# Another order of all operations in a scheduled kernel: pooled attention and a gated-convolution feed-forward on one core

## The chip, the core and the metric

The kernel runs on one core of a Trainium2 chip. The core has a matrix engine (TensorE, PE in the profile; PEld is its weight load), a vector engine (VectorE, DVE), a scalar engine (ScalarE, ACT), a general engine (GpSimd, POOL) and a sync engine (SyncE, SP) that here only issues DMAs. Each engine takes its instructions in the order in which they were written, and waits on semaphores where it needs another's result. The metric is the device time of one execution in microseconds (us); lower is better.

## What is computed

The input has 8 batches, 8 heads, 576 rows and 64 columns per head. Keys and values are averaged over 8 neighbouring rows, so that 72 are left; then follow the softmax attention and a feed-forward net whose gate is a convolution over 3 rows:

```python
k_p = k.reshape(B, H, Sp, pool, D).mean(axis=3)
v_p = v.reshape(B, H, Sp, pool, D).mean(axis=3)
scores = scale * np.matmul(q, k_p.transpose(0, 1, 3, 2))
attn = np.exp(scores - np.max(scores, axis=-1, keepdims=True))
attn = attn / (np.sum(attn, axis=-1, keepdims=True) + 1e-09)
x = np.matmul(attn, v_p)                    # heads joined: (8, 576, 512)
h = np.maximum(x @ w_in, 0.0)               # 512 -> 1024
conv_out = sum over k of conv_w[k] * h shifted by k - 1 rows
out = (h * sigmoid(conv_out)) @ w_out       # 1024 -> 512, f32
```

## The kernel before

**Tiling.** The batches go in pairs, as groups 0 to 3. A group has nine attention tiles of 128 rows (group 0 has ten). A tile runs through this chain: scores on PE (lines 607 and 620), the row maximum on DVE (633), its subtraction on DVE (645; for group 0 on PE, 653), the exponential on ACT (682), a transpose of the weights (groups 0 and 1 on PE, 692, with a copy; groups 2 and 3 by a DMA transpose that SyncE issues, `att_send`, 701), the product with the values on PE (717), the reciprocal of the sums on DVE (730), the division on ACT or DVE (738, 745), and a transpose of the result (on PE, 762, with a copy, 770; for the later batches by DMA, `att_out`, 754).

**Feed-forward.** Per batch PE multiplies by w_in in eight blocks fb of 128 columns, each in two halves (775); ACT takes the relu (784). The convolution is made on PE for some blocks (939) and for the rest, in batches 4 to 7, by taps on DVE (911) with the tanh on ACT (921). Taps need a halo: for these batches the first and last rows of pairs of blocks are copied by POOL or ACT (`ffn_wrap`, 859 and 860). DVE makes the gate (979, 981) and multiplies by h, four blocks at once (`ffn_times`, 989). Then PE multiplies by w_out, per tile in two halves (997); ACT or DVE copies the PSUM bank to memory (`ffn_copy`, 1008) and a DMA of two parts of 128 KB stores it (`ffn_store`, 1020), from SyncE or, for some tiles of group 3, from ACT.

**Loads.** SyncE and ACT load the first pieces of batch 0, which are cast by ACT or DVE (306). All the other loads are issued by POOL, which casts on the way: queries (284, into one of four buffers qp), keys by pairs of batches (291, into the only buffer kk), values (317 and 320, into three buffers v), w_in (327) and w_out (335). Values and keys are then pooled on DVE (511, 515, 464) and keys on PE (431, 470, 493). Queries are transposed on PE (541, with a copy, 559), except those of batches 6 and 7: these go through a DMA transpose that SyncE issues (`q_send`, 553).

**Spare matmuls.** `fill` (424) multiplies constants and writes to a PSUM bank that nobody reads.

**What sets the order.** All operations are made first, as a list, with their buffers left open. `Graph.order` (line 164) then walks a table of numbers, `ORDER`: a negative number takes a spare matmul, another number n takes operation n // 2 on the first or second of its possible engines, by n % 2. Two more tables are read along the way: `FORMS` (the shape in which an operation uses the matrix array) and `PLACES` (the buffer or bank that each result takes). The operations are emitted in this order, so it is the order of the instructions on each engine, and it also sets which buffer is reused when. The tables are constants; no planner runs.

## Time and profile before

| | us |
|---|---|
| three runs, median (lowest to highest) | 213.52 (213.04 to 213.94) |
| the profiled execution | 213.68 |
| its span, first to last instruction or transfer | 211.7 |
| PE busy | 198.9 |
| DVE busy | 190.5 |
| ACT busy | 167.2 |
| POOL busy | 36.7 |

The profile's time axis begins with the span, and all times of instructions below are on it. Busy time counts an engine's instructions, not their issue of DMAs. PE has work from 2.8 to 205.9 us. A row of a group gives the line, the engine, the operation, what it writes and reads, and a count; then the busy time, the mean of one in ns and the idle time ahead of them, with what ended it.

### The profile page before, as it was taken

The numbers are of one execution on the slowest core, as the hardware profiler recorded it, in microseconds if no ns is written. First come the engines' busy times: TensorE is split into PE (matmuls) and PEld (weight loads), VectorE is DVE, ScalarE is ACT, GpSimd is POOL, SyncE is SP. The second block draws the span as 40 slices with busy tenths as digits, with TensorE's granted clock in tenths as the row PEclk, the third lists the DMA queues.
The fourth block names the chain that finished last, engine by engine and source line by source line (L and its number), as shares of the span: only waits on it lengthen the run. The fifth ranks groups of instructions, "written<-read, shape, count | busy, mean of one in ns | idle before, by whom it ended". The sixth has DMA issues, their size and how long they took to land.

```text
span 211.7 us, 6644 instructions
## 1 busy us (share of the span) xinstructions
PE 198.9 (94%) x2726; PEld 136.4 (64%) x2746; DVE 190.5 (90%) x338; ACT 167.2 (79%) x345; POOL 36.7 (17%) x60
## 2 busy tenths in 40 slices
PE   4899999999999999999999899999999999999990
PEld 1468788765688876776778675666666656654450
DVE  7879988999999999999998989999999999999520
ACT  2558677998999869999979977989899997889030
POOL 8604630052131110200000021000014400202000
PEclk9999999999999999999999999999999999999997
DMA  6999999999999999879663646756646626204985
GB/s 212 222 205 206 208 206 208 208 207 205 208 206 208 202 179 202 177 139 156 130 92 69 147 96 78 173 104 151 122 96 133 113 64 149 53 0 103 261 259 171
DMA packets 48834, 33.47 MB, mean 158 GB/s; under 512 B 28300, under 2 KB 43812, under 8 KB 48804
## 3 DMA queue, kind: packets, MB, share of 16 engines
q0 software_dynamic: 15216, 15.40, 44.6%
q1 hardware_dynamic: 32432, 15.93, 35.9%
q10 hardware_dynamic: 1156, 1.72, 2.8%
q8 instruction: 21, 0.34, 0.6%
q14 instruction: 9, 0.07, 0.1%
HBM read 32.52 MB, written 9.44 MB: 198 GB/s over the span
## 4 chain that ended last, share of the span: by engine, by line
PE 68%; DVE 19%; issue 5%; ACT 4%; DMA 2%; DVEq 0%; ACTq 0%
PE psum L997 25%; PE psum L775 22%; PE psum L717 5%; PE psum L939 3%; DVE negm L633 3%; DVE v L511 2%; PE psum L692 2%; DMA eT<-e 2%; PE psum L424 2%; DVE sd L645 2%; DVE gT L981 2%; PE psum L620 2%; DVE gT L989 1%; PE psum L653 1%; PE psum L762 1%
## 5 line engine op out<-in xcount | busy, mean ns | idle before, releaser
L775 PE MATMUL psum<-xT,w_in_sb 128*128 128x288 bf16 x512 | 72.0, 286 | 0.2
L997 PE MATMUL psum<-w_out_sb,gT 128*128 128x512 bf16 (+1 forms) x276 | 65.6, 373 | 1.4 <-issue 0.6
L775 PEld LDWEIGHTS <-w_in_sb 128*128 128x128 bf16 x512 | 47.8, 98 | 15.3
L784 ACT ACTIVATE hT<-psum 128x576 bf16<-128x576 f32 x64 | 41.1, 669 | 8.0 <-PE psum L775 7.8
L997 PEld LDWEIGHTS <-gT 128*128 128x128 bf16 x296 | 27.5, 98 | 26.5 <-DVE gT L989 0.5
L633 DVE TENSOR_REDUCE negm<-psum 128x8 f32<-128x576 f32 (+2 forms) x37 | 27.4, 750 | 2.0 <-ACT e L682 0.9
L921 ACT ACTIVATE gT<-tg,ratio 128x576 bf16<-128x576 f32 x28 | 21.6, 795 | 2.2 <-DVE tg L911 2.1
L911 DVE SCALAR_TENSOR_TENSOR tg<-hT,ratio,tg 128x576 f32<-128x576 bf16 x28 | 22.3, 813 | 0.7
L911 DVE SCALAR_TENSOR_TENSOR tg<-hT,ratio 128x576 f32<-128x576 bf16 x28 | 22.2, 812 | 0.2 <-ACT gT L921 0.2
L859 POOL COPY hT<-hT 128x126 bf16<-128x126 bf16 x7 | 5.7, 808 | 93.8 <-ACT hT L784 74.9
L989 DVE TENSOR_TENSOR gT<-gT,hT 128x2304 bf16<-128x2304 bf16 x16 | 21.6, 1354 | 0.2
L645 DVE TENSOR_TENSOR sd<-psum,negm 128x576 f32<-128x576 f32 x27 | 19.9, 751 | 0.6
L717 PE MATMUL psum<-vm,eT 128*128 128x65 bf16 (+5 forms) x240 | 19.0, 222 | 0.9 <-DMA eT<-e 0.9
L738 ACT ACTIVATE x<-psum,r 128x64 bf16<-128x64 f32 (+1 forms) x80 | 17.6, 352 | 2.8 <-DVE r L730 2.7
L682 ACT ACTIVATE e<-sd 128x576 bf16<-128x576 f32 x27 | 18.6, 703 | 0.4 <-DVE sd L645 0.2
L745 DVE TENSOR_TENSOR x<-psum,r 128x512 bf16<-128x512 f32 (+1 forms) x27 | 18.2, 682 | 0.5
L717 PEld LDWEIGHTS <-eT 128*128 128x128 bf16 (+1 forms) x240 | 15.1, 100 | 5.3 <-DMA eT<-e 1.7
L939 PE MATMUL psum<-hT,dw 64*64 64x288 bf16 (+2 forms) x576 | 17.0, 256 | 0.3 <-ACT qT L559 0.2
L939 PEld LDWEIGHTS <-dw 64*64 64x64 bf16 x576 | 13.9, 107 | 3.4 <-issue 2.3
L424 PE MATMUL psum<-gT 128*128 128x448 bf16 x40 | 13.1, 433 | 3.2 <-DVE gT L1106 2.8
L1008 ACT COPY osb<-psum 128x512 f32<-128x512 f32 x24 | 14.3, 600 | 1.2 <-PE psum L997 1.2
L511 DVE TENSOR_TENSOR v<-v 128x1280 bf16<-128x1280 bf16 (+2 forms) x24 | 12.9, 538 | 0.2
(95 smaller groups left out, 244.8 us busy)
## 6 DMA issues: line engine op xcount, KB each, us to landing
out_dram<-osb SPq DMA_DIRECT2D x54, 128.0 KB, 2.5
v<-in_v_dram POOLq DMA_DIRECT2D x8, 512.0 KB, 12.6
qp<-in_q_dram POOLq DMA_DIRECT2D x7, 576.0 KB, 15.3
kk<-in_k_dram POOLq DMA_DIRECT2D x3, 1152.0 KB, 13.7
out_dram<-qp ACTq DMA_DIRECT2D x12, 128.0 KB, 3.4
hT<-in_k_dram SPq DMA_DIRECT2D x2, 576.0 KB, 5.2
w_in_sb<-in_moe_w_in_dram POOLq DMA_DIRECT2D x2, 512.0 KB, 13.7
w_out_sb<-in_moe_w_out_dram POOLq DMA_DIRECT2D x1, 1024.0 KB, 23.7
```

The source lines that it names most:

```text
L633: nc.vector.tensor_reduce(out=a["m"][0:rows], in_=a["s"][0:rows, :, 0:2 * KW].rearrange("p a (h s) -> p a h s", s=Sp), axis=AX.X, op=OP.ma ...
L645: nc.vector.tensor_tensor(out=a["d"][0:rows], in0=a["s"][0:rows, :, 0:2 * KW].rearrange("p a (h s) -> p a h s", s=Sp), in1=a["m"][0:rows]. ...
L682: nc.scalar.activation(out=dst, in_=src, func=ACT.Exp,)
L717: nc.tensor.matmul(out=a["o"][lo:hi, h // 4, (h % 4) * (D + 1):(h % 4 + x1 - x0) * (D + 1)], lhsT=a["eT"][:, j, lo:hi], rhs=buf("vm", b)[: ...
L745: nc.vector.tensor_tensor(out=a["x"][0:rows].rearrange("p (a h d) -> p a h d", a=2, d=D), in0=ov[:, :, :, 0:D], in1=r[0:rows].unsqueeze(3) ...
L775: nc.tensor.matmul(out=banks(ps)[:, j, 0:SC], lhsT=w_in_block(dc, fb), rhs=buf("xT", g)[:, dc, i * S + j * SC:i * S + (j + 1) * SC], start ...
L784: nc.scalar.activation(out=h_of(b)[:, fb].rearrange("p (a s) -> p a s", a=2), in_=banks(ps)[:, :, 0:SC], func=ACT.Relu, scale=1.0 if (b, f ...
L911: nc.vector.scalar_tensor_tensor(out=acc, in0=h, scalar=w, in1=acc if tap else mid, op0=OP.mult, op1=OP.add)
L921: nc.scalar.activation(out=gate, in_=acc_of(b, fb, ps), func=squash(b, fb), scale=ratio[:, 1, fb:fb + 1])
L939: nc.tensor.matmul(out=banks(pss[r ^ c])[c * D:(c + 1) * D, j, lo:hi], lhsT=dw[r * D:(r + 1) * D, tap * n_fb + fb, :], rhs=hT[r * D:(r + 1 ...
L989: nc.vector.tensor_tensor(out=gate, in0=gate, in1=h_of(b)[:, four], op=OP.mult)
L997: nc.tensor.matmul(out=bank(ps)[0:rows, columns], lhsT=buf("gT", g)[:, fb, t * P:t * P + rows], rhs=w_out_sb[:, fb, columns], start=(fb == 0),
```

## The change

The three tables `ORDER`, `FORMS` and `PLACES` have other values; everything else is the same. Both versions of `ORDER` have 1077 entries, 40 of them spare matmuls. 38 operations are on another engine: DVE makes two fewer copies of transposed queries and eight instead of five of the late copies of the output, which ACT loses, and the two casts of batch 0's raw keys are swapped between ACT and DVE; the rest are single small operations. Some operations have another form, so that PE has 2740 matmuls instead of 2746. The first lines of the table, as the diff has them:

```diff
-        0, 12, 10, 24, 16, 4, 44, 28, 8, 36, 14, 32, 46, 19, -1, -1, -1, -1, 21, 7,
-        -1, -1, -1, 42, 48, 26, 34, 38, 64, 2, -1, -1, -1, 40, -1, -1, -1, -1, -1, 114,
-        102, 108, 118, 122, 126, 104, 117, 113, 111, 107, 120, 292, 128, 125, -1, -1, -1, 66, 68, 358,
...
+        0, 12, 10, 24, 16, 4, 44, 28, 8, 36, 14, 32, 46, 42, 40, 3, 48, 26, -1, 38,
+        19, 66, -1, -1, -1, 64, 34, 6, 68, -1, -1, 21, -1, -1, 74, -1, -1, -1, 114, 102,
+        107, 118, 104, 108, 111, 113, -1, -1, -1, 116, 120, 292, 294, 58, 122, 126, -1, 296, -1, 125,
...
```

What it moves is seen in the instructions of each engine. Names are buffers with their numbers; x2 is two instructions of one kind.

**The start, on ACT.** The first instructions of ACT before; kk0 takes the raw keys of batch 0 (staged in hT0), qp2 its raw queries (staged in hT1):

```order
L1116 ACT_TABLE_LOAD
L1116 CAST gT1_122<-ident_62 128x128
L324 DMA gT1_122<-in_moe_conv_w_dram 24x128
L306 CAST qp2_76<-hT1_117 128x2x256 x2
L306 CAST kk0_78<-hT0_116 128x1152
L559 COPY qT0_79<-psum_61 128x2x256
L456 CAST kT0_82<-psum_61 64x2x72 x3
L559 COPY qT0_79<-psum_61 128x2x320
L682 ACTIVATE e3_101<-psum_61 128x576
```

and now:

```order
L1116 ACT_TABLE_LOAD
L1116 CAST gT1_122<-ident_62 128x128
L324 DMA gT1_122<-in_moe_conv_w_dram 24x128
L306 CAST kk0_78<-hT0_116 128x1152
L306 CAST qp2_76<-hT1_117 128x2x256 x2
L456 CAST kT0_82<-psum_61 64x2x72 x3
L559 COPY qT2_81<-psum_61 128x2x320
L682 ACTIVATE e2_100<-psum_61 128x2x2x144
L682 ACTIVATE e0_98<-psum_61 128x576
```

ACT's cast of keys stands ahead of its casts of queries, and it is now the first half of the keys; DVE's is the second. On PE eleven spare matmuls stand ahead of the first transposes of queries, before it were fifteen, and on DVE the six memsets of the buffers e stand behind the constants that the keys' pooling needs.

**The late loads on POOL and the transposes on SyncE, from about 55 to 120 us.** POOL's last loads before: the values of batch 5, the queries of 7, the values of 6, the keys of group 3, the values of 7 (two rows to a load of values):

```order
L317 DMA v1_88<-in_v_dram 128x4x512
L320 DMA v1_88<-in_v_dram 64x512
L284 DMA qp1_75<-in_q_dram 128x4x576
L317 DMA v0_87<-in_v_dram 128x4x512
L320 DMA v0_87<-in_v_dram 64x512
L291 DMA kk0_78<-in_k_dram 128x9x512
L317 DMA v2_89<-in_v_dram 128x4x512
L320 DMA v2_89<-in_v_dram 64x512
```

Ahead of them stand the queries of batch 6, the values of batch 4 and the queries of batch 5. Now, from the values of batch 5 on: the values of 5 and 6, the queries of 5, the keys of group 3, the queries of 7, the values of 7, and last the queries of 6:

```order
L317 DMA v0_87<-in_v_dram 128x4x512
L320 DMA v0_87<-in_v_dram 64x512
L317 DMA v1_88<-in_v_dram 128x4x512
L320 DMA v1_88<-in_v_dram 64x512
L284 DMA qp1_75<-in_q_dram 128x4x576
L291 DMA kk0_78<-in_k_dram 128x9x512
L284 DMA qp0_74<-in_q_dram 128x4x576
L317 DMA v2_89<-in_v_dram 128x4x512
L320 DMA v2_89<-in_v_dram 64x512
L284 DMA qp3_77<-in_q_dram 128x4x576
```

The values of batch 6 come ahead of the queries of batch 7, and the queries of batch 6, which were loaded ahead of the values of batch 4, are the last load of all.

SyncE's first instructions behind the loads of batch 0, before; line 553 is a transpose of queries (batch 7, then batch 6), line 701 of softmax weights (group 2's tiles 1, 2, 3 and 7), line 754 of an attention result, line 1020 a store of group 0:

```order
L553 DMA_TRANSPOSE qT2_81<-qp1_75 128x18x128
L701 DMA_TRANSPOSE eT1_105<-e5_103 128x5x128
L1020 DMA out_0_dram<-osb1_124 64x512 x2
L1020 DMA out_0_dram<-osb4_127 64x512 x2
L701 DMA_TRANSPOSE eT2_106<-e3_101 128x5x128
L1020 DMA out_0_dram<-osb0_123 64x512 x2
L1020 DMA out_0_dram<-osb4_127 64x512 x2
L701 DMA_TRANSPOSE eT1_105<-e0_98 128x5x128
L553 DMA_TRANSPOSE qT0_79<-qp0_74 128x18x128
L701 DMA_TRANSPOSE eT2_106<-e1_99 128x5x128
L754 DMA_TRANSPOSE xT0_114<-x3_110 128x4x128
```

and now (line 701: tiles 1, 2, 3, 0 and 4 of group 2):

```order
L1020 DMA out_0_dram<-osb3_126 64x512 x2
L1020 DMA out_0_dram<-osb1_124 64x512 x2
L1020 DMA out_0_dram<-osb0_123 64x512 x2
L701 DMA_TRANSPOSE eT1_105<-e0_98 128x5x128
L701 DMA_TRANSPOSE eT2_106<-e3_101 128x5x128
L553 DMA_TRANSPOSE qT2_81<-qp0_74 128x18x128
L553 DMA_TRANSPOSE qT0_79<-qp3_77 128x18x128
L701 DMA_TRANSPOSE eT0_104<-e1_99 128x5x128
L701 DMA_TRANSPOSE eT2_106<-e2_100 128x5x128
L701 DMA_TRANSPOSE eT1_105<-e5_103 128x5x128
L754 DMA_TRANSPOSE xT0_114<-x0_107 128x4x128
```

Both transposes of queries stand now one behind the other, behind those of tiles 1 and 2 and three stores, and ahead of those of tiles 3 and 0; before, that of batch 7 was the first of all, and that of batch 6 came behind tile 3's.

**The end, on DVE and ACT.** The last instructions of DVE before; line 989 is the last two products of batch 7, line 1008 copies of output tiles, qp and osb are the buffers of the copies:

```order
L911 SCALAR_TENSOR_TENSOR tg2_120<-hT0_116,ratio_71,tg2_120 128x576
L911 SCALAR_TENSOR_TENSOR tg0_118<-hT0_116,ratio_71 128x576
L911 SCALAR_TENSOR_TENSOR tg1_119<-hT0_116,ratio_71 128x576
L911 SCALAR_TENSOR_TENSOR tg0_118<-hT0_116,ratio_71,tg0_118 128x576
L911 SCALAR_TENSOR_TENSOR tg1_119<-hT0_116,ratio_71,tg1_119 128x576
L989 TENSOR_TENSOR gT1_122<-gT1_122,hT0_116 128x4x576 x2
L1008 COPY qp2_76<-psum_61 128x512
L1008 COPY osb0_123<-psum_61 128x512
L1008 COPY osb1_124<-psum_61 128x512
L1008 COPY qp0_74<-psum_61 128x512
L1008 COPY qp0_74<-psum_61 128x256 x2
```

and now:

```order
L911 SCALAR_TENSOR_TENSOR tg1_119<-hT0_116,ratio_71 128x576
L911 SCALAR_TENSOR_TENSOR tg1_119<-hT0_116,ratio_71,tg1_119 128x576
L989 TENSOR_TENSOR gT1_122<-gT1_122,hT0_116 128x4x576 x2
L1008 COPY qp0_74<-psum_61 128x512
L1008 COPY osb2_125<-psum_61 128x512
L1008 COPY osb3_126<-psum_61 128x512
L1008 COPY osb0_123<-psum_61 128x512
L1008 COPY qp0_74<-psum_61 128x512
L1008 COPY qp3_77<-psum_61 128x512
L1008 COPY osb4_127<-psum_61 128x512
L1008 COPY qp3_77<-psum_61 128x512
L1008 COPY qp0_74<-psum_61 128x256 x2
```

Eight whole tiles and the two halves of the last tile are copied on DVE behind the last products, instead of four and the two halves. The last instructions of ACT before:

```order
L1008 COPY qp3_77<-psum_61 128x512
L1020 DMA out_0_dram<-qp3_77 64x512 x2
L1020 DMA out_0_dram<-qp2_76 64x512 x2
L1020 DMA out_0_dram<-qp3_77 64x512 x2
L1008 COPY qp3_77<-psum_61 128x512
L1008 COPY qp1_75<-psum_61 128x512
L1020 DMA out_0_dram<-qp3_77 64x512 x2
L1008 COPY qp2_76<-psum_61 128x512
L1020 DMA out_0_dram<-qp2_76 64x512 x2
L1008 COPY qp3_77<-psum_61 128x512
L1020 DMA out_0_dram<-qp3_77 64x512 x2
L1020 DMA out_0_dram<-qp0_74 64x256 x2
```

and now:

```order
L1008 COPY qp3_77<-psum_61 128x512
L1008 COPY osb1_124<-psum_61 128x512
L1020 DMA out_0_dram<-qp2_76 64x512 x2
L1020 DMA out_0_dram<-qp3_77 64x512 x2
L1020 DMA out_0_dram<-qp0_74 64x512 x2
L1008 COPY qp2_76<-psum_61 128x512
L1020 DMA out_0_dram<-qp0_74 64x512 x2
L1020 DMA out_0_dram<-qp3_77 64x512 x2
L1020 DMA out_0_dram<-qp2_76 64x512 x2
L1008 COPY qp0_74<-psum_61 128x512
L1020 DMA out_0_dram<-qp0_74 64x512 x2
L1020 DMA out_0_dram<-qp0_74 64x256 x2
```

Behind the last tanh (line 921) ACT copied five tiles and issued six whole pairs of stores and a half one; now it copies four and issues seven and a half, some of them for tiles that DVE copied. On SyncE the stores of tiles 8 and 1 of group 1 now come well ahead of the last products, and behind them stand stores only of tiles that DVE or ACT copies behind these products.

More of the change, by code (lines that the diff above doesn't have):

```diff
@@ L72 @@
     ORDER = (
[54 rows of a table removed]
[54 rows of a table added]
     )
     FORMS = (
-        0, 0, 0, 0, 1, 1, 1, 1, 0, 0, 0, 0, 0, 1, 1, 0, 1, 1, 0, 0, 1, 0, 1, 0, 0, 0, 0, 1, 0, 0, 0, 1, 1, 1, 1, 1, 1, 1, 0, 1,
+        1, 0, 0, 0, 1, 1, 1, 1, 0, 0, 0, 0, 0, 1, 0, 0, 1, 0, 0, 0, 0, 0, 1, 1, 0, 0, 0, 1, 0, 0, 0, 1, 1, 1, 1, 1, 1, 1, 1, 1,
     )
     PLACES = (
[18 rows of a table removed]
[18 rows of a table added]
     )
```

138 rows, old and new, of tables (ORDER, PLACES) are left out of this document.

## The prediction

> **What bounds the kernel now.** I read the head of the page first, then its chain, and the windows of the two ends.
>
> ```profile
> span 211.7 us, 6644 instructions
> PE 198.9 (94%) x2726; PEld 136.4 (64%) x2746; DVE 190.5 (90%) x338; ACT 167.2 (79%) x345; POOL 36.7 (17%) x60
> ...
> PE   4899999999999999999999899999999999999990
> ...
> PE 68%; DVE 19%; issue 5%; ACT 4%; DMA 2%; DVEq 0%; ACTq 0%
> ```
>
> PE is 94% busy and 68% of the chain of work that ended last; DVE, 90% busy, is 19%. So the time is PE's work plus what PE waits. An order moves work; it takes none away. What it can gain is therefore small and lies in a few places: the start, single waits, and the end behind the last matmul. What it can lose is not small, as DVE has only a tenth of its time to spare. The profiled execution took 213.68 us, 211.7 of span and 1.98 around it; the median shown is 213.52, so I subtract 0.16 at the end. A measurement of this kernel tells about 0.5% (1.1 us) from no change.
>
> **The start.** The timeline of the first 12 us, piece by piece:
>
> ```profile
> 2.79 5.61 PE L424 MATMUL psum<-gT 128*128 128x448 bf16 x15 [2.79 <-DVE gT L1106]
> ...
> 6.05 1.14 ACT L306 CAST qp<-hT 128x512 bf16<-128x512 f32 x2 [3.66 <-DMA hT<-in_q_dram]
> ...
> 8.40 0.98 DVE L306 CAST kk<-hT 128x1152 bf16<-128x1152 f32 x1
> 8.62 1.15 ACT L306 CAST kk<-hT 128x1152 bf16<-128x1152 f32 x1 [1.43 <-DMA hT<-in_k_dram]
> 9.44 1.14 PEld L431 LDWEIGHTS <-kk 128*64 128x64 bf16 x36 [0.86 <-DVE kk L306]
> 9.44 1.32 PE L431 MATMUL psum<-gT,kk 128*64 128x144 bf16 x36 [0.70 <-DVE kk L306]
> ```
>
> PE fills its time with 15 spare matmuls until 8.3 us and then waits for the first half of the keys, which DVE casts late (8.40, behind its constants) although ACT idles for 3.66 us ahead of its first cast. Now ACT casts that half first, and DVE, with the six small memsets moved behind, the other half. The first 18 of the 36 pooling matmuls can then stand ahead of 9.44, and only 18 are left behind the second cast: 1.32 / 2 = 0.66 us earlier, and up to 1.1 with the shorter copies of the transposed queries. The four spare matmuls that went from this place come again later: both orders hold 40, so they cost the same 13.1 us in all unless they fill time in which PE would wait. I take **−0.5** (0 to −1.1), since behind the first scores PE leans on DVE again, which gains less.
>
> **The stall at 120 us.** From the chain in order of time, and from the waits of 95 to 125 us:
>
> ```profile
> 117.05 4.37 DMA eT<-e
> ...
> PEld L717 <- DMA eT<-e: 1.7, 2, 1.2
> ...
> PE psum L717 <- DMA eT<-e: 0.9, 1, 0.9
> ```
>
> One transpose of softmax weights (tile 6 of group 2) goes out at 117.05 and lands 4.37 us later; PE loses 0.9 us on it. In the new order that tile's scores stand earlier on PE, and between its transpose and its use lie 1 to 3 us more. I take **−0.7** (0 to −0.9).
>
> **The query transposes.** SyncE's timeline and what the page of the line says on landing, then the loads beside them on POOL:
>
> ```profile
> 72.83 3.64 SPq L553 DMA_TRANSPOSE qT<-qp  x1
> 81.29 1.20 SPq L701 DMA_TRANSPOSE eT<-e  x1
> ...
> 95.28 1.23 SPq L701 DMA_TRANSPOSE eT<-e  x1
> 96.61 3.66 SPq L553 DMA_TRANSPOSE qT<-qp  x1
> 100.44 1.20 SPq L701 DMA_TRANSPOSE eT<-e  x1
> ```
>
> ```profile
> DMA to landing us min/median/max: 5.5/7.4/9.2
> ```
>
> ```profile
> 73.51 1.15 POOL L291 DMA_DIRECT2D kk<-in_k_dram  x1 [9.46 <-DVE xT L770]
> 85.91 0.77 POOL L317 DMA_DIRECT2D v<-in_v_dram  x1 [11.24 <-DVE vm L515]
> ```
>
> ```profile
> kk<-in_k_dram POOLq DMA_DIRECT2D x1, 1152.0 KB, 12.0
> ```
>
> The queries of batch 7 go out at 72.83, beside the last key load (73.51, 12.0 us to landing), and take 9.2 us; those of batch 6, at 96.61 with no load in flight, take 5.5. So a large load beside a transpose costs 9.2 − 5.5 = 3.7 us of landing. The new order issues both transposes back to back after the last loads: that removes this collision. But nothing waited at 82 us for batch 7's queries, which belong to the last group: no PE wait names them. What it adds is a queue. Each takes SyncE 3.65 us to issue, 7.3 together, and behind them now stand the transposes of tiles 3 and 0 of group 2; before, tile 3 went out ahead of the second query transpose, at 95.28.
>
> The loads decide when they may start. The value load of batch 7 now waits for batch 4's values (DVE, 2.5 us earlier than before: about 83 instead of 85.9), and the query load of batch 6 stands last, behind it. The value load took 5.9 us to land before; two of such a size behind one another, issued at 83 to 84, land by 92 to 94. Then 92 to 94 plus 3.65 (batch 6) plus 1.2 issue and 2.6 landing (tile 3, the shortest landing of that line) gives 99.5 to 101.5, and tile 0 comes about 1.2 us later. Where PE wants them shows in the rows of the values there:
>
> ```profile
> 99.77 0.53 PE L717 MATMUL psum<-vm,eT 128*128 128x130 bf16 x6
> 100.14 4.08 PE L775 MATMUL psum<-xT,w_in_sb 128*128 128x288 bf16 x32
> ...
> 107.91 0.30 PE L717 MATMUL psum<-vm,eT 128*128 128x130 bf16 x2
> ```
>
> 99.77 is tile 3 now, 107.91 tile 0. In the new order they stand third and fifth in the run of products that begins at 100.14, each place 4.08 / 8 = 0.51 us: at 101.2 and 102.2. The slack is between −0.3 and 1.7 us for tile 3 (tile 0 has 0.2 less), and a start that is 0.5 earlier on PE takes half a microsecond of it. Bounds: 0, when the loads land at 92; +3.7, when the collision of the row above returns here. I take **+0.8**, nearer to the lower end since the load's own row, 5.9, is the nearest.
>
> **Waits for POOL at the end of the taps.** The late halo copies:
>
> ```profile
> 190.02 0.88 POOL L859 COPY hT<-hT 128x126 bf16<-128x126 bf16 x1 [8.88 <-issue]
> 190.85 0.81 POOL L860 COPY hT<-hT 128x126 bf16<-128x126 bf16 x1
> ```
>
> A pair takes 1.64 us from end to end on POOL. In the new order the pair for blocks 4 and 5 of batch 7 is this last one, its relu is emitted just ahead of it, and the taps of these blocks stand close behind on DVE; ACT's tanh and then DVE's last products queue behind them. Bounds 0 (two taps of 0.8 us cover it) and +1.6 (nothing does). The rest of the middle comes out even by my count of the work ahead of each landmark (within half a microsecond on DVE, ACT and PE). I take **+0.4**.
>
> **The end.** Windows (PE, PEld, DVE, ACT, POOL, granted clock, DMA share, GB/s), then the end of the chain and the stores:
>
> ```profile
> 180.00:192.00 12.00, 11.95 (x70) 6.81 (x70) 11.79 (x16) 9.66 (x19) 2.78 (x4) 1.00 0.10 23
> ...
> 196.00:206.00 10.00, 9.82 (x52) 4.92 (x51) 4.08 (x7) 2.24 (x4) 0.00 (x0) 1.00 0.89 262
> 206.00:210.00 4.00, 0.00 (x0) 0.00 (x0) 0.34 (x1) 0.00 (x0) 0.00 (x0) 0.94 0.81 244
> ```
>
> ```profile
> 197.49 8.40 PE psum L997 x46
> ...
> 205.91 0.42 DVE qp L1008
> ```
>
> ```profile
> 192.06 8.41 SPq L1020 DMA_DIRECT2D out_dram<-osb  x12
> ```
>
> ```profile
> GB/s 0 0 0 0 0 48 212 205 197 216 227 205 194 361 231 309 235 205 302 302 302 220 294 261 231 317 238 279 231 231 298 246 309 268 255 106 93 15 0 0
> ...
> out_dram<-osb SPq DMA_DIRECT2D x14, 128.0 KB, 3.3
> out_dram<-qp ACTq DMA_DIRECT2D x12, 128.0 KB, 3.4
> ```
>
> PE ends at 205.89, the last copy at 206.33, and the span at 211.7: between them the DMA still moves 244 GB/s. From 196 on the queues are full (0.89), while from 180 to 192 they idle (0.10). The end is thus bound by data: a tile is 0.262 MB, one per microsecond at 262 GB/s. In the order before, SyncE feeds stores from 192.06 on without a break, and twelve tiles are left at 196.0, so about 208 to 210. In the new order SyncE's stores of tiles 8 and 1 of group 1 are out by 191; the copies of tiles 4, 8 and 5 of group 2 stand on DVE behind the last product (which ended at 196.99 before), and ACT's first stores behind its last three tanh. By my reading 14 tiles are issued from 196.5 on: 14 x 1.0 us from about 197.0 is 211.0, against 210.1 as the last data now: **+0.9**. Bounds: −0.5, if the products end that much sooner and nothing else binds, and +1.2, if the first store comes at 197.3.
>
> A rate above this row would undo the term. The Trainium skill, "DMA: Bandwidth & Descriptors", section "Specifications", gives a core's limit to memory as about 358 GB/s; by it fourteen tiles would take 10.3 us, an estimate, and the term would be nothing. The same page ("Issuing engines are not separate DMA queues") has all issuers share the same 16 engines, so the second queue would not raise the rate; the trace agrees, with 262 GB/s while both queues issue.
>
> **Sum.** −0.5 − 0.7 + 0.8 + 0.4 + 0.9 = +0.9; 213.68 + 0.9 = 214.6 on the profiled execution's scale, less 0.16: **214.4 us**, with 213.2 to 215.8 for this case alone.
>
> **Rivals.**
>
> *The queue on SyncE holds PE* (slower, 216.8). One mechanism: batch 6's query transpose waits for its load, the load lands after 95 instead of 92 to 94, and tiles 3 and 0 of group 2 queue behind it; each microsecond later is one that PE stands still near 101 us, and DVE and ACT behind it get no work back. For it: the 9.2 us of the transpose beside a load, 12.0 us of the load. Against it: the smaller load is the only one then in flight. Price: the term rises from 0.8 to the 3.2 that lies between its ends and the 3.7, that is 214.4 + 2.4 = 216.8.
>
> *The end is hidden and the gains come in full* (faster, 211.9). Products end sooner, stores keep above 262 GB/s, and the new place of the transposes costs nothing: −1.0 − 0.9 + 0 + 0.3 + 0 = −1.6, so 211.9. For it: slices of the end that reach 302 to 361 GB/s in the row above (190 to 212 us in 40 slices), and the removed collision. Against it: 0.89 busy at 262 is the mean over 10 us. The Trainium skill's page named above, section "Rules for kernel authors", says that a transpose beside ordinary DMAs needs nothing; by it the transposes would never be late. Here the two landings, 9.2 and 5.5 us, speak against it as a rule on time.
>
> *The order does nothing that can be measured* (213.5): PE has the same products to make, and the waits change places.
>
> **How the numbers follow.** Forecast 0.42, queue 0.27, faster rival 0.26, nothing 0.05. Within 0.5% is 212.45 to 214.59. The forecast's own spread gives 0.20 to same, 0.20 to slower, 0.02 to faster; the faster rival 0.24 and 0.02; the queue 0.27 slower; the last 0.05 same. So faster 0.26, same 0.27, slower 0.47. The range goes from 211.4 to 217.4: it takes in the middles of both rivals and leaves a tenth at each side.
>
> **What would show it.** Start: the pooling matmuls of line 431 begin near 7.5 us, and the first scores before 11.2. Stall: no wait of line 717 for a transpose near 120. Queue: line 717's waits for eT near 101, under 1 us in the forecast and 2 to 4 in the slower rival. Taps: ACT's last tanh wait for POOL's copies. End: DMA share under 0.2 from 191 to 196, a span that ends 5 us or more behind the last matmul. I am wrong if PE waits somewhere that I have counted as even, from 20 to 95 us above all, where DVE is full and both orders differ in detail.

## The result and the profile after

| | before | after |
|---|---|---|
| median of four runs, us (lowest to highest) | 213.73 (213.04 to 213.99) | 220.81 (220.28 to 223.00) |
| the profiled execution, us | 213.68 | 223.00 |
| its span, us | 211.7 | 221.3 |
| ratio of the runs, 95% interval | | 1.0364 (1.0324 to 1.0405) |

The new order is 7.1 us slower by the medians, outside the predicted range. The profiled execution is the slowest of the four, so its losses below are about 2 us larger than the median's. Where single executions of a run below were disturbed (the 220.41 of e8_before_start), its ratio leaves them out.

The page of the changed kernel (busy times, 40 slices of PE and of its granted clock, chain):

```profile
span 221.3 us, 6641 instructions
PE 202.4 (91%) x2721; PEld 138.0 (62%) x2740; DVE 192.9 (87%) x341; ACT 167.2 (76%) x342; POOL 34.1 (15%) x60
...
PE   4799999989999999887799999999999999999970
...
PEclk9999999999999999999589999999999999999997
...
PE 77%; DVE 9%; DMA 7%; issue 3%; ACT 1%; DVEq 0%
```

PE has one new hole, in slices 17 to 20 (88 to 111 us), and in slices 20 and 21 the granted clock falls to 5 and 8 tenths. Elsewhere PE's row differs by a tenth at most, but for the end. The chain of work that ended last now has 7% of DMA instead of 2%. The windows of that place, before and then after (PE, PEld, DVE, ACT, POOL busy; clock; DMA share; GB/s):

```profile
90.00:100.00 10.00, 9.71 (x182) 6.58 (x184) 9.77 (x20) 9.36 (x23) 0.00 (x0) 1.00 0.86 144
100.00:110.00 10.00, 9.84 (x141) 7.38 (x141) 9.75 (x18) 8.08 (x20) 0.00 (x0) 1.00 0.70 121
110.00:120.00 10.00, 9.89 (x229) 8.11 (x224) 9.12 (x18) 9.25 (x18) 0.00 (x0) 1.00 0.50 98
```

```profile
90.00:100.00 10.00, 7.95 (x141) 5.40 (x142) 7.89 (x17) 6.97 (x12) 0.00 (x0) 1.00 1.27 193
100.00:110.00 10.00, 6.96 (x88) 4.72 (x86) 5.42 (x13) 5.13 (x14) 0.00 (x0) 0.79 1.04 161
110.00:120.00 10.00, 9.90 (x160) 6.77 (x163) 8.26 (x13) 7.46 (x18) 0.00 (x0) 0.87 0.40 85
```

PE is busy for 29.44 us of these thirty before and 24.81 after: 4.6 us of idleness are added. The busy time is also slower: 6.96 at 0.79 and 9.90 at 0.87 of the clock are worth (0.21 x 6.96) + (0.13 x 9.90) = 2.8 us less. Together 7.4 of the span's 9.6 us. A row of 0.79 or 0.87 is a mean of two values, as shorter windows show:

```profile
104.00:106.00 2.00, 0.00 (x0) 0.00 (x0) 0.00 (x0) 0.35 (x1) 0.00 (x0) 0.95 0.77 89
106.00:112.00 6.00, 5.30 (x29) 3.80 (x30) 3.43 (x9) 3.61 (x16) 0.00 (x0) 0.50 0.74 161
112.00:114.00 2.00, 1.95 (x11) 1.03 (x10) 1.95 (x3) 0.97 (x4) 0.00 (x0) 0.85 0.46 90
```

The clock is halved for (0.05 x 2 + 0.50 x 6 + 0.15 x 2) / 0.5 = 6.8 us, from about 105.8, while PE still waits, to 112.6. This stretch isn't in every execution. The mean granted clock of the four was 0.978, 0.990, 0.982 and 0.991, at 223.00, 220.33, 221.28 and 220.28 us; e1 below, whose trace has no such stretch, has 0.990. So the two at 220.3 had little or none of it (their traces were not read), and of the median's 7.1 us the clock is about 0.5 (220.81 − 220.3), an estimate.

The waits of 85 to 115 us name the cause of the rest, and SyncE's timeline shows where it comes from:

```profile
PE psum L717 <- DMA eT<-e: 4.0, 2, 3.0
...
PE psum L939 <- issue: 0.8, 1, 0.8
```

```profile
87.58 5.12 SPq L701 DMA_TRANSPOSE eT<-e  x2
92.88 8.90 SPq L553 DMA_TRANSPOSE qT<-qp  x2
101.88 4.34 SPq L701 DMA_TRANSPOSE eT<-e  x3
```

The transposes of tiles 1 and 2 go out at 87.58, those of the queries at 92.88, and tile 3's only at 101.88, as PE waits 3.0 us for it. The landing times of the first two lines, that of batch 6's query load, and that load's issue on POOL:

```profile
DMA to landing us min/median/max: 9.5/9.5/9.5
```

```profile
DMA to landing us min/median/max: 12.1/12.1/12.1
...
84.56 0.77 POOL L284 DMA_DIRECT2D qp<-in_q_dram  x1
```

Tiles 1 and 2 take 9.5 us to land (2.6 to 5.0 in this place before), and batch 6's queries, issued at 84.56, land at 84.56 + 12.1 = 96.6. The end, first two windows, then the last of PE's product rows:

```profile
200.00:206.00 6.00, 5.95 (x28) 2.60 (x28) 5.96 (x8) 3.18 (x5) 0.00 (x0) 1.00 0.41 94
206.00:214.00 8.00, 8.00 (x46) 4.21 (x44) 4.70 (x8) 0.67 (x2) 0.00 (x0) 1.00 0.87 238
```

```profile
195.66 18.44 PE L997 MATMUL psum<-w_out_sb,gT 128*128 128x512 bf16 x91
```

The queues are at 0.41 from 200 to 206 us and at 0.87 from then on. PE ends at 214.10, 7.2 us ahead of the span's end; before, 205.89 and 5.8.

### The profile page after: what moved, and what is told of

It reads as the page before. It is cut to its first block, busy times and chain, and to the rows that moved or that the text cites. A ratio compares the mean times of both kernels' runs of the same rounds, so it can differ in the third digit from the quotient of the medians.

```text
span 221.3 us, 6641 instructions
## 1 busy us (share of the span) xinstructions
PE 202.4 (91%) x2721; PEld 138.0 (62%) x2740; DVE 192.9 (87%) x341; ACT 167.2 (76%) x342; POOL 34.1 (15%) x60
## 4 chain that ended last, share of the span: by engine, by line
PE 77%; DVE 9%; DMA 7%; issue 3%; ACT 1%; DVEq 0%
PE psum L775 27%; PE psum L997 26%; DMA eT<-e 7%; PE psum L717 6%; PE psum L939 5%; PE psum L424 3%; PE psum L692 2%; PE psum L620 2%; PE psum L762 2%; PE psum L607 2%; DVE negm L633 1%; PE psum L653 1%; PE psum L541 1%; PE psum L545 1%; DVE kT L339 1%
## 5 line engine op out<-in xcount | busy, mean ns | idle before, releaser
L775 PE MATMUL psum<-xT,w_in_sb 128*128 128x288 bf16 x512 | 73.5, 292 | 0.4 <-DVE x L745 0.2
L775 PEld LDWEIGHTS <-w_in_sb 128*128 128x128 bf16 x512 | 49.1, 100 | 17.3 <-issue 0.9
L859 POOL COPY hT<-hT 128x126 bf16<-128x126 bf16 x7 | 3.2, 461 | 103.4 <-ACT hT L784 85.1
L1008 ACT COPY osb<-psum 128x512 f32<-128x512 f32 x23 | 13.8, 613 | 3.2 <-PE psum L997 3.0
L730 DVE RECIPROCAL r<-psum 128x8 f32<-128x8 f32 (+1 forms) x37 | 7.2, 199 | 7.7 <-PE psum L717 6.9
```

The lines of the kernel that those rows point to most:

```text
L775: nc.tensor.matmul(out=banks(ps)[:, j, 0:SC], lhsT=w_in_block(dc, fb), rhs=buf("xT", g)[:, dc, i * S + j * SC:i * S + (j + 1) * SC], start ...
```

## The experiments

The theories. **Queue:** the two query transposes take SyncE's time ahead of tiles 3 and 0, whatever else is in flight. **Late loads:** the same transposes cost little; they and the weights' transposes are slow because the loads of batch 7's values and batch 6's queries are still in flight. **Clock:** a part of the loss is the granted clock behind PE's wait. **Data at the end:** the tail is longer since more tiles are left to store behind the last products; its rival is the time that the issue of these stores takes. All medians, each with those of the kernel before on the same chip:

| run | us (lowest to highest) | before, us | ratio (95%) |
|---|---|---|---|
| e1_q6_early | 217.32 (216.88 to 217.70) | 213.11 | 1.0191 (1.0164 to 1.0218) |
| e2_send_behind | 219.50 (218.49 to 220.72) | 213.11 | 1.0296 (1.0250 to 1.0342) |
| e3_before_sends | 219.73 (219.22 to 220.10) | 213.11 | 1.0303 (1.0273 to 1.0332) |
| e4_fills | 221.75 (218.27 to 222.63) | 213.11 | not separable |
| e5_early_behind | 219.36 (218.25 to 220.21) | 213.29 | 1.0263 (1.0226 to 1.0301) |
| e6_stores | 219.03 (218.30 to 220.37) | 213.29 | 1.0270 (1.0237 to 1.0304) |
| e7_before_late_load | 213.56 (213.01 to 214.47) | 213.29 | 1.0011 (0.9994 to 1.0028) |
| e8_before_start | 212.61 (212.31 to 220.41) | 213.29 | 0.9969 (0.9953 to 0.9986) |
| e9_b7_first | 230.15 (229.32 to 230.75) | 213.31 | 1.0801 (1.0739 to 1.0863) |
| e10_tail | 215.64 (215.34 to 217.34) | 213.31 | 1.0128 (1.0066 to 1.0190) |
| e11_before_b7 | 215.12 (214.53 to 216.51) | 213.31 | 1.0092 (1.0067 to 1.0117) |
| e12_b7_first_late_load | 228.21 (227.03 to 230.07) | 213.31 | 1.0709 (1.0628 to 1.0789) |
| e13_b7_behind | 218.45 (216.78 to 219.64) | 213.08 | 1.0250 (1.0202 to 1.0298) |
| e14_sends_fills | 218.04 (217.47 to 218.41) | 213.08 | 1.0234 (1.0199 to 1.0268) |
| e15_before_two | 213.43 (212.06 to 218.74) | 213.08 | 1.0001 (0.9971 to 1.0031) |
| e16_no_late_loads | 215.21 (214.71 to 215.98) | 213.08 | 1.0112 (1.0071 to 1.0154) |

The edits are shown as the rows of the engine that they move, against the kernel named.

### e1_q6_early: the late query load put back early

The kernel after, on POOL; qp_77 takes batch 6's queries, v_89 first batch 4's values and then 7's.

```diff
 L291 DMA kk_78<-in_k_dram 128x9x512
+L284 DMA qp_77<-in_q_dram 128x4x576
 L317 DMA v_89<-in_v_dram 128x4x512
...
 L317 DMA v_89<-in_v_dram 128x4x512
 L320 DMA v_89<-in_v_dram 64x512
-L284 DMA qp_77<-in_q_dram 128x4x576
```

> The changed kernel with one edit: POOL issues the load of batch 6's queries right behind the keys of group 2, where the kernel before has it, instead of last. Theory L (the late load): it is this load, in flight from 84.6 to 96.6, that holds the transposes of tiles 1 and 2 of group 2 (9.5 us and more to landing) and then batch 6's query transpose, and all that PE loses near 100 us (0.9 + 3.0 us of waits and the slow clock behind them) goes: 213 to 215.5 us. Rival S (SyncE's queue): two query transposes of 3.65 us ahead of tile 3's weights hold PE whatever is loaded: 217 us or more, with line 717 still waiting over 2 us near 102. Rival O (the rest of the order): the waits go but the time comes back elsewhere in DVE's work: 217 or more without such waits.

It took 217.32, which is 3.5 us less than the kernel after. The windows, the wait, and SyncE:

```profile
90.00:100.00 10.00, 8.82 (x149) 5.99 (x150) 8.89 (x18) 7.16 (x13) 0.00 (x0) 1.00 1.12 215
100.00:110.00 10.00, 8.46 (x107) 5.86 (x107) 7.95 (x17) 8.46 (x26) 0.00 (x0) 1.00 0.87 133
```

```profile
91.13 7.68 SPq L553 DMA_TRANSPOSE qT<-qp  x2
98.91 4.41 SPq L701 DMA_TRANSPOSE eT<-e  x3
```

PE's wait for eT fell from 4.0 to 1.5 us and the clock stayed at 1.00. The time lies above Theory L's range, and the wait is below the 2 us of Rival S: both were right in part. One load of 576 KB less at this place is thus worth half of the loss, although neither engine order nor SyncE's order changed. The rest stayed: the value load of batch 7 is still in flight, and the two query transposes still take 7.68 us of SyncE.

### e2_send_behind: batch 6's transpose behind tiles 3 and 0

The kernel after, on SyncE; qT_79 is batch 6's, qT_81 batch 7's.

```diff
 L553 DMA_TRANSPOSE qT_81<-qp_74 128x18x128
-L553 DMA_TRANSPOSE qT_79<-qp_77 128x18x128
 L701 DMA_TRANSPOSE eT_104<-e_99 128x5x128
 L701 DMA_TRANSPOSE eT_106<-e_100 128x5x128
+L553 DMA_TRANSPOSE qT_79<-qp_77 128x18x128
```

> The changed kernel with one edit: SyncE issues batch 6's query transpose behind the weights of tiles 3 and 0 of group 2 instead of ahead of them; the loads stay. Theory L says that the load itself collides: tiles 1 and 2 still land after 9 us and PE still waits about 0.9 us for tile 2, but tile 3 goes out at about 99 and lands by 102, when PE wants it, so the 3.0 us and most of the slow clock go: 214 to 216.5 us. Rival S expects the same of tile 3, and nothing left at tiles 1 and 2: 213 to 214. Rival O: 217 or more.

At 219.50 it gained 1.3 us by the medians, in the range of Rival O only. SyncE shows why:

```profile
92.82 8.24 SPq L553 DMA_TRANSPOSE qT<-qp  x1
101.17 2.58 SPq L701 DMA_TRANSPOSE eT<-e  x2
```

A single query transpose now holds SyncE for 8.24 us, as long as both did: while the late load is in flight, the issue itself is stretched. The transpose that blocked was batch 7's, not batch 6's.

### e3_before_sends and e11_before_b7: the queue alone, in the order before

e3 moves both transposes behind tile 2's, e11 only batch 7's (the first + and its -); the loads are those of before.

```diff
-L553 DMA_TRANSPOSE qT_81<-qp_75 128x18x128
 L701 DMA_TRANSPOSE eT_105<-e_103 128x5x128
...
 L701 DMA_TRANSPOSE eT_106<-e_101 128x5x128
+L553 DMA_TRANSPOSE qT_81<-qp_75 128x18x128
+L553 DMA_TRANSPOSE qT_79<-qp_74 128x18x128
 L1020 DMA out_dram<-osb_123 64x512 x2
 L1020 DMA out_dram<-osb_127 64x512 x2
 L701 DMA_TRANSPOSE eT_105<-e_98 128x5x128
-L553 DMA_TRANSPOSE qT_79<-qp_74 128x18x128
```

> The kernel before with one edit: both query transposes stand together behind the weights of tile 2 of group 2, with the loads as before, so no load is in flight beside them (the last lands at 92.1). Rival S: 92.6 plus 7.3 us of issue holds tile 3 to 99.9 and its landing to 102.6, where PE wants it at 99.8: a wait of 2.8 us and one or two more by a slow clock, 216.5 to 219. Theory L: transposes without a load beside them land quickly and the queue costs what the issue takes, at most the 2.8 us: 214.5 to 216.5, no slow clock. If the time stays within 213 to 214.3, neither the queue nor the issue time is what holds PE.

> The kernel before with one edit: batch 7's query transpose goes from the first place on SyncE (72.8 us) to the place behind tile 2's weights (92.6). Loads and all else stay. Theory Q: its 3.65 us of issue now stand in the stretch in which SyncE has no gap, tile 3 goes out at about 99 instead of 95.3 and lands after 101.5, where PE wants it at 99.8, and what stands behind comes late too: 215.5 to 218.5 us. If it stays within 213 to 214.3, the place of batch 7's transpose alone costs nothing.

e3 took 219.73, 6.6 us more than before. SyncE, the wait and the window:

```profile
92.97 6.36 SPq L553 DMA_TRANSPOSE qT<-qp  x2
99.38 2.52 SPq L1020 DMA_DIRECT2D out_dram<-osb  x4
101.99 2.58 SPq L701 DMA_TRANSPOSE eT<-e  x2
```

```profile
PE psum L717 <- DMA eT<-e: 4.9, 1, 4.9
```

```profile
100.00:110.00 10.00, 5.35 (x29) 3.70 (x30) 5.23 (x10) 4.18 (x12) 0.00 (x0) 0.66 0.71 151
```

So the queue can cost as much by itself, here with two pairs of stores (2.52 us) behind the transposes and ahead of tile 3. e11 took 215.12, 1.8 us more than before (just below its Theory Q), and its wait is just as long:

```profile
PE psum L717 <- DMA eT<-e: 1.8, 1, 1.8
```

With one transpose in the queue the clock stayed at 1.00 and the loss is the wait; with two the wait is 4.9 and the loss 6.6. The difference is the question of the next two runs.

### e4_fills and e14_sends_fills: the clock

Spare matmuls on PE, ahead of tile 3's products with the values, where PE waits: this pair of rows twelve times in the kernel after (e4), and 22 times in e3's order (e14).

```diff
+L424 LDWEIGHTS gT_122
+L424 MATMUL psum<-gT_122 128x448
```

> The changed kernel with 12 more spare matmuls (about 0.2 us each) right ahead of the values of tile 3 of group 2, where PE idles 3.0 us. They compute nothing that is read. Theory C (clock): the products behind the wait take 0.96 us a half block instead of 0.49 because the granted clock falls after the idle time; PE that stays busy keeps the clock, and the eight slow halves give back about 3.7 us: 216.5 to 218.5 us. Rival: the products are slow for another reason (transfers beside them, weights that come late), and the spare matmuls only fill time that was lost: 220 to 221.5.

> The kernel before with both query transposes behind tile 2's weights (219.7 us; PE idles 4.9 us ahead of tile 3's values, the granted clock of 100 to 110 us falls to 0.66 and 32 products take 5.9 us instead of 4.1), and 22 spare matmuls in that idle time. They compute nothing that is read. Theory C (clock): the clock stays at 1.00 and 1.5 to 3 us come back: 216.7 to 218.2. Rival: the products are slow for another reason, or the stall just moves: 219 or more.

e4's four runs scatter from 218.27 to 222.63, so its time told nothing; in its trace the clock is 1.00 in all windows from 90 to 120 us. e14 took 218.04 against e3's 219.73; by the ratios to before, (1.0303 − 1.0234) x 213.1 = 1.5 us less, though it issues more work. Its window:

```profile
100.00:110.00 10.00, 9.50 (x79) 5.96 (x81) 5.74 (x11) 5.61 (x15) 0.00 (x0) 1.00 0.68 142
```

The clock is 1.00 where e3 had 0.66. The clock's part of e3's loss is thus about 1.5 us, and with the wait of 4.9 that is 6.4 of the 6.6 found. The same product of 16 matmuls, in the chain of the kernel after and in that of e1, shows what it means for a row:

```profile
109.14 3.72 PE psum L775 x16
```

```profile
105.47 1.96 PE psum L775 x16
```

### e5_early_behind and e13_b7_behind: looking for a place on SyncE

e5 is e1 with batch 6's transpose behind that of tile 4. e13 is e10 (below) with batch 6's first, then tiles 3, 0, 4 and 7, then batch 7's:

```diff
-L553 DMA_TRANSPOSE qT_81<-qp_74 128x18x128
 L553 DMA_TRANSPOSE qT_79<-qp_77 128x18x128
 L701 DMA_TRANSPOSE eT_104<-e_99 128x5x128
 L701 DMA_TRANSPOSE eT_106<-e_100 128x5x128
 L701 DMA_TRANSPOSE eT_105<-e_103 128x5x128
+L701 DMA_TRANSPOSE eT_106<-e_102 128x5x128
+L553 DMA_TRANSPOSE qT_81<-qp_74 128x18x128
```

> The changed kernel with both edits: the load of batch 6's queries behind the keys of group 2, and SyncE's transpose of these queries behind the weights of tiles 3, 0 and 4 of group 2. If load and queue are all that holds PE near 100 us, no wait of line 717 over 0.5 us is left there, and the 1.7 us that tile 3 still cost with the early load goes: 215.0 to 216.2 us. What is left over the kernel before (1.5 to 2.5 us) is then the rest of the order: a gap of 0.9 us near 92 and the later stores at the end. If PE stands as before, a third thing holds tile 3.

> The changed kernel with the early load of batch 6's queries and the changed end, and SyncE in another order: batch 6's query transpose, the weights of tiles 3, 0, 4 and 7 of group 2, then batch 7's query transpose, so that one and not two of them stands ahead of tile 3 and none ahead of what PE wants by 112. Theory Q: the 1.7 us of wait for tile 3 go and do not come back at tile 7: 213.7 to 214.8 us, against 215.6 with both ahead. Rival: what stands behind batch 7's transpose (results of group 2) is late in its turn: 215.2 or more.

Both lost against the kernels that they were made from (219.36 against 217.32, 218.45 against 215.64). In e5's trace (an execution of 220.06 us) the wait, 2.8 us, moved to tile 7, whose transpose now stands behind batch 6's, and the clock fell to 0.86 in 110 to 120:

```profile
110.00:120.00 10.00, 7.19 (x129) 5.17 (x126) 5.91 (x11) 4.80 (x8) 0.00 (x0) 0.86 0.62 93
```

In e13 batch 6's transpose, now ahead of the tiles, stands still for PE, and the results' transposes (line 754) come late behind batch 7's. SyncE's wait:

```profile
SPq L553 <- PE psum L997: 7.4, 1, 7.4
```

DVE waits 1.3 us for a buffer that a transpose of results still reads. SyncE idles in its wait and is short of time right behind. Neither order found a place that costs nothing; I tried no third one.

### e6_stores and e10_tail: the end

e6 is e5 with one more pair of stores given from ACT to SyncE. e10 is e1 with the copies of tiles 7 and 8 of group 2 on ACT three tanh earlier, and their stores moved up on SyncE:

```diff
 L1008 COPY qp_76<-psum 128x512
+L1008 COPY osb_124<-psum 128x512
+L1008 COPY osb_126<-psum 128x512
 L921 ACTIVATE gT_122<-tg_120,ratio 128x576
 L921 ACTIVATE gT_122<-tg_118,ratio 128x576
 L921 ACTIVATE gT_122<-tg_119,ratio 128x576
 L1008 COPY qp_77<-psum 128x512
-L1008 COPY osb_124<-psum 128x512
```

> As the one with both edits, and at the end the store of tile 1 of group 3 goes from ACT to SyncE, so that ACT has one pair of stores less ahead of its last copy (tile 7), which also takes a buffer that no earlier store holds. Theory I (issue): the end is bound by ACT's queue, which issues three pairs of stores of 1.6 us ahead of that copy and makes the last stores late; 0.8 to 1.5 us less than the other. Theory D (data): the DMA is full there and the end comes no sooner: within 0.4 us of the other.

> The changed kernel with the early load of batch 6's queries and another end: ACT copies tiles 7 and 8 of group 2, which PE has long made, 4 us ahead of the last products, and SyncE stores them then. Theory D (data): the end is bound by what is left to store behind the last products, about 1 us for each tile, and two tiles fewer give 1.2 to 2 us against the 217.3 of the early load alone: 215.3 to 216.1. Rival: the copies hold ACT's last tanh and the products come later, or the end is bound by the last tile's own chain: within 0.5 us of 217.3.

e6 changed nothing that can be told (219.03 against 219.36), and its trace has the same 7.3 us from PE's end to the span's end as e5's (216.6 − 209.35 and 218.4 − 211.06). e10 took 215.64 against 217.32: 1.7 us for two tiles stored ahead of the last products. Their tails, e1's and then e10's last products (start, length) beside their spans of 215.7 and 213.8:

```profile
195.72 12.61 PE L997 MATMUL psum<-w_out_sb,gT 128*128 128x512 bf16 x64
```

```profile
195.72 12.83 PE L997 MATMUL psum<-w_out_sb,gT 128*128 128x512 bf16 x66
```

From PE's end to the span's end e1 has 215.7 − 208.33 = 7.4 us and e10 213.8 − 208.55 = 5.3, with PE ending at the same time. So each tile stored ahead of the last products takes about 1 us off the end, and one pair of stores less in ACT's queue takes nothing off.

### e7_before_late_load: the late load alone

The kernel before, with batch 6's queries as the last load (issued at about 87):

```diff
-L284 DMA qp_74<-in_q_dram 128x4x576
 L317 DMA v_89<-in_v_dram 128x4x512
 L320 DMA v_89<-in_v_dram 64x512
...
 L317 DMA v_89<-in_v_dram 128x4x512
 L320 DMA v_89<-in_v_dram 64x512
+L284 DMA qp_74<-in_q_dram 128x4x576
```

> The kernel before with one edit: POOL issues the load of batch 6's queries last, behind the values of batch 7 (at about 87 instead of 46 us). SyncE's order stays, with tile 3's weights ahead of these queries. Theory L: the transposes of tiles 2 (91.3) and 3 (95.3) run beside the load and land 9 us after their issue, tile 3 at 104 where PE wants it at 99.8: 217 to 220 us. Rival S: without two query transposes ahead of tile 3 a late load costs at most half a microsecond: 213 to 214.3.

At 213.56 it costs nothing that can be told from noise. In SyncE's order of before no query transpose is issued while the load is in flight (86.70 to 95.4), only those of tile 2 (90.83) and, at its very end, of tile 3 (95.05). They land in 5.3 and 4.9 us instead of 2.6 and 4.4, and PE's longest wait for them is 0.7 us. A late load alone is not the cause; it needs the transposes beside it.

### e8_before_start and e15_before_two: the start by itself

The kernel before, with ACT casting the first half of the keys first:

```diff
+L306 CAST kk_78<-hT_116 128x1152
 L306 CAST qp_76<-hT_117 128x2x256 x2
-L306 CAST kk_78<-hT_116 128x1152
```

e15 adds a store of group 0 moved behind the transposes of tiles 8 and 6.

> The kernel before with the start's edit alone: ACT casts the first half of batch 0's keys ahead of its other casts, DVE the second half. The first scores come 0.6 us earlier. If PE's path carries it to the end, as the prediction's first term has it: 0.4 to 0.7 us faster. Rival: the first 40 us are bound by the loads at 206 GB/s and by DVE, and PE, which is filled there with spare matmuls, gives the gain back: within 0.25 us of the kernel before.

> The kernel before with the start's edit (212.6 us alone) and with SyncE's store of tile 4 of group 0 behind instead of ahead of the weights of tiles 8 and 6 of group 2, so that tile 6 goes out 1.2 us earlier and PE's wait of 0.9 us at 121 goes. If both terms reach the end: 211.6 to 212.2 us. Rival: tile 6's transpose is held by something else than SyncE's queue, or PE's gain is lost later: 212.4 to 212.9.

e8 took 212.61: 0.7 us faster (0.3 to 1.0 by its interval). Its first scores stand at 11.15 us instead of 11.71, so the gain of the start reaches the end. It has the lowest median of this study. e15 scattered, from 212.06 to 218.74, above both of its ranges in the median, and doesn't show even e8's gain (1.0001), although it has the same edit; why is open.

### e9_b7_first and e12_b7_first_late_load: a query transpose beside the loads

If the queue was the trouble, batch 7's transpose should go first of all, as it did before. e9 is e1 with its load moved behind the values of batch 4 and its transpose ahead of SyncE's stores; e12 is the same with the late query load kept.

```diff
 L299 DMA hT_116<-in_k_dram 128x2x576
+L553 DMA_TRANSPOSE qT_80<-qp_74 128x18x128
 L1020 DMA out_dram<-osb_126 64x512 x2
...
 L701 DMA_TRANSPOSE eT_106<-e_101 128x5x128
-L553 DMA_TRANSPOSE qT_81<-qp_74 128x18x128
 L553 DMA_TRANSPOSE qT_79<-qp_77 128x18x128
```

> The changed kernel with the early load of batch 6's queries and, besides, batch 7's queries loaded behind the values of batch 4 and transposed by SyncE ahead of all else, at about 70 us, where SyncE idles (its buffer changes places with that of batch 5's, so that it is free by 66). Batch 6's transpose stays ahead of tile 3. Theory Q (SyncE's time): from 83 to 125 us SyncE has no gap, so each of the two 3.65 us transposes pushes all behind it; with batch 7's out of this stretch tile 3 goes out by 97 and lands by 100, and no wait of line 717 over 0.5 us is left: 214.3 to 216 us. Rival: the wait moves on once more, as it did when batch 6's transpose went behind tile 4: over 217.

> As the one with batch 7 first, but with the load of batch 6's queries last, as the changed kernel has it. Theory L: the late load still holds the transposes of tiles 1 and 2 beside it for 9 us and batch 6's transpose behind it, and with it tile 3: 217.5 us or more. Theory Q: with SyncE's time free, only what the load itself delays is left, at most 1 us over the run with both early: 214.5 to 217.

Far slower than before and than Theory Q in both: 230.15 and 228.21. SyncE, the wait and the windows of e9:

```profile
67.86 10.43 SPq L553 DMA_TRANSPOSE qT<-qp  x1
```

```profile
DVE kk L464 <- DMA kk<-in_k_dram: 11.7, 1, 11.7
```

```profile
70.00:80.00 10.00, 10.00 (x169) 8.16 (x159) 9.71 (x19) 9.04 (x19) 1.01 (x1) 1.00 1.27 153
80.00:90.00 10.00, 6.55 (x127) 4.38 (x125) 4.71 (x8) 6.33 (x11) 1.32 (x2) 1.00 1.40 124
```

Beside the loads, the one transpose takes 10.43 us to issue and 22.7 to land. The load of group 3's keys takes 22.5 us (10.1 after), and DVE waits 11.7 us for it. The engines' share is 1.27 to 1.40 (1.23 at 206 GB/s from 40 to 60 us of this trace), while the rate falls to 153 and 124 GB/s. The collision works both ways. PE itself then waits at line 939, 4.4 us and 5.5 us, and the clock falls to 0.66 from 100 to 110. That e12, with the late load, is no slower than e9 speaks for the early transpose, and not that load, as what costs here.

### e16_no_late_loads: the transposes without the loads

The kernel after, without the loads of batch 7's values and batch 6's queries; the results of these batches are computed from what lies in the buffers. Its line numbers are higher by four.

```diff
 def load_q(b):
+    if b == 6:
+        return
 def load_v(b):
+    if b == 7:
+        return
```

> The changed kernel without the loads of batch 7's values and batch 6's queries (what lies in their buffers is used instead, so the output of these batches isn't the reference's): no load is in flight behind 85 us. Theory L (collision): the transposes of tiles 1 and 2 land in 3 us, both query transposes are issued from 90 on, tile 3 is out by 97.5, and PE waits at most 0.5 us: 214.8 to 216 us. Theory Q: 7.3 us of issue ahead of tile 3 stay, so 216.5 to 217.5, as with the early load.

It took 215.21: 1.12% above before instead of 3.64%. PE and SyncE:

```profile
90.00:100.00 10.00, 9.99 (x199) 6.75 (x197) 9.86 (x20) 8.28 (x14) 0.00 (x0) 1.00 0.96 157
100.00:110.00 10.00, 9.46 (x127) 6.72 (x116) 8.91 (x17) 9.18 (x27) 0.00 (x0) 1.00 0.73 132
```

```profile
90.66 6.40 SPq L557 DMA_TRANSPOSE qT<-qp  x2
97.16 4.70 SPq L705 DMA_TRANSPOSE eT<-e  x3
```

With the same order on every engine but POOL, tiles 1 and 2 land in 3.7 us, tile 3 goes out at 97.16 instead of 101.88, and PE loses 0.5 us instead of 5 of these twenty. So in this order the late loads are what makes the queue late: (1.0364 − 1.0112) x 213.7 = 5.4 us of the loss. The queue theory by itself fails here; it holds in e3, where the stores stand ahead of tile 3 too. PE ends at 206.02 us, 0.1 later than before; of the 1.5 us by which this span is longer, 1.4 are the tail (213.2 − 206.02 = 7.2 us, 5.8 before).

## Why the prediction was wrong, step by step

**The failed step is the query transposes**, forecast at +0.8 with an upper bound of 3.7. It rests on "two of such a size behind one another, issued at 83 to 84, land by 92 to 94". The values did (their second part 84.0 + 7.9 = 91.9), the queries came at 96.6. That alone would be the condition of the slower rival, "lands after 95". But it did not work as the rival says: batch 6's transpose never waited for its load. Batch 7's, ahead of it, was issued at 92.88 beside that load, and its issue took 6.09 us where the row of before has 3.65 and e11, with no load beside it, 2.71. Tile 3 went out at 101.88, took 4.8 us to land (2.6 in the prediction) and was used at 106.70, against 99.5 to 101.5. A load was priced as a time after which the transposes may start, and it is a neighbour that slows them, and the tiles' transposes of 87.6 as well (9.5 us instead of 2.6 to 5.0). When a load stretches the issue, and how far, is not settled: the transpose of 72.83 in the trace of before took 3.64 us, although the DMA engines carried 211 GB/s from 70 to 73 us.

**The bound was too low for the wait and left out two things.** PE's waits for eT are 0.93 and 3.04, 4.0 us together, just above the bound. To them came 0.84 us of "issue" near 92 (0.9 in e1, gone in e16, so perhaps of the load of batch 7's values; its path is not shown) and, in the profiled execution, 2.8 us of clock. The prediction said that DVE and ACT would get no work back, and was right in that, but took PE's work behind the wait at full speed. Over the runs, waits of 1.5 us (e1) and 1.8 (e11) left the clock at 1.00; 2.8 (e5), 3.0 (after) and 4.9 (e3) brought stretches at 0.50 of 3.4, 6.8 and 6.8 us, worked out as above. The Trainium skill, "TensorE: Matmul & The Clock Gate", section "HAM oscillation — how this bites in real kernels", gives the rule that idle gaps of PE should stay under about 3.4 us, since it is throttled behind longer ones. These rows agree in kind; here the clock falls behind waits of 2.8 and 3.0 us already.

**The collision that the change was said to remove** (at 73 to 82) was real but cost PE nothing, as the prediction also said; the change moved it to a place where a tile waits behind it. The rule of the Trainium skill, "DMA: Bandwidth & Descriptors", section "Rules for kernel authors", that a transpose beside ordinary DMAs needs nothing, stands there beside a warning of corrupted data and does not hold for time here: tiles 1 and 2 landed in 9.5 instead of 3.7 us in this very order, and a query transpose took 22.7 in e9.

**Start:** −0.5 forecast, −0.66 measured (e8, 0.31% of 213.3). PE's first pooling products begin at 7.51 as foretold, the first scores at 10.96 instead of 11.71:

```profile
7.51 0.75 PE L431 MATMUL psum<-gT,kk 128*64 128x144 bf16 x18 [0.16 <-DVE gT L359]
...
10.96 0.37 PE L607 MATMUL psum<-kT,qT 64*64 64x72 bf16 x16
```

**The stall at 120:** gone; no wait of PE for a transpose is left behind 115 us, and PE is busy for 9.98 us of 120 to 130 (9.03 before). Right as a step, but little of its 0.9 us arrives at the end: by the products that both traces share, PE is about 8.4 us late at 120 and 8.2 late at its end. Something of 0.7 us is lost behind 120, which I did not find.

**The waits for POOL** (+0.4): ACT waits longer for taps (3.6 us from 180 on, 1.9 before), and what it waits for is DVE, not POOL's copies as the sign had it. From the last product of line 989 to PE's end both have 8.9 us. Not separated by any run.

**The middle:** "comes out even" was not right. By 89 us the lead of 0.75 has become 0.3 to 0.6 us of delay.

**The end:** +0.9 forecast, 7.2 − 5.8 = 1.4 measured, but not by the mechanism given; that the size came near was luck. The term counted 14 tiles where before twelve were left. From the last product of line 989 to the span's end (before 197.00, after 205.22) the traces move 14.70 x 233 = 3.43 MB and 16.08 x 214 = 3.44 MB, 13 tiles each. What differs is how the stores start:

```profile
197.00:200.00 3.00, 2.94 (x14) 1.39 (x15) 1.84 (x3) 0.00 (x0) 0.00 (x0) 1.00 0.89 269
197.00:211.70 14.70, 8.82 (x48) 4.62 (x48) 3.42 (x6) 2.24 (x4) 0.00 (x0) 0.92 0.77 233
```

```profile
205.22:208.22 3.00, 3.00 (x15) 1.37 (x15) 2.53 (x5) 0.59 (x1) 0.00 (x0) 1.00 0.80 177
205.22:221.30 16.08, 8.88 (x49) 4.59 (x48) 5.91 (x10) 1.17 (x2) 0.00 (x0) 0.91 0.76 214
```

The queues idled just ahead (0.41, where the sign was under 0.2) and the first 3 us move (269 − 177) x 3 = 0.28 MB less, about 1 us of stores at the 262 GB/s of before. e10 takes the loss back by storing two tiles earlier (1.7 us).

**The sum by the runs:** 5.4 (late loads, e16) and 1.7 (end, e10) less 0.7 (start, e8) is 6.4 of 7.1 to 7.8 us (medians and ratio). They were measured in different orders, so adding them up is an estimate. The rest is the 0.5 us of PE's wait left in e16 and what stays open above.

## What to carry to other kernels

When a DMA transpose is moved, ask what is in flight at its new place, not only when its input has landed: a load beside it can stretch its issue and its landing, and can itself be stretched, and everything behind it on the queue pays. When a wait of 2 us or more is added to PE, price the slower clock behind it too: here up to 2.8 us on 4 us of waits, in one execution and not in the next. Where a kernel stores to the last microsecond, keep the queues busy up to the last product: each tile stored ahead of it took about 1 us off here. And when the profiled execution is the slowest of several, compare the mean clocks before its losses are taken for the kernel's.

## What the runs showed of the hardware

A query transpose (576 KB) held SyncE for 2.7 us with little beside it, 3.65 twice in the trace of before (once beside loads), and 6.1, 8.24 and 10.43 beside loads elsewhere, so the duration of an issue is no constant of the instruction. With transposes and loads together the DMA engines were busier (1.40) and moved less (124 GB/s, 80 to 90 us of e9) than with loads alone (1.24 at 207 GB/s from 40 to 60 us of before). The granted clock of PE was 1.00 or 0.50, in stretches of 3.4 or 6.8 us; values between are means over a window. A transposed tile of weights lands in 2.6 us at best and in 9.5 beside these loads.
